# q loaded a batch ahead, gate stores from ScalarE's queue, and the second phase's weights in chunks

## The chip, the cores and the metric

The kernel runs on one core of a Trainium2 chip. TensorE (PE) multiplies, VectorE (DVE), ScalarE (ACT) and GpSimd (POOL) work elementwise, SyncE (SP) issues DMA transfers; ScalarE can issue them as well. The metric is the device time of one launch in microseconds. Kernels are compared by the median of several runs.

## The reference

Three layers follow each other over 8 batches of 576 tokens with 512 channels: linear attention in 8 heads with an RMS norm, a channel mix with a token shift and a squared ReLU, and causal attention in four experts of which two are chosen per token.

```python
kv  = einsum('bhsd,bhse->bhde', k, v)            # 64 x 64 per head
out = einsum('bhsd,bhde->bhse', q, kv)
x   = out / sqrt(mean(out*out) + 1e-6) * g_norm  # heads side by side: 512
xk  = mu_k * x + (1 - mu_k) * x_prev             # x_prev: x shifted by a token
xr  = mu_r * x + (1 - mu_r) * x_prev
k   = maximum(xk @ w_k, 0)                       # 512 -> 1024
x   = sigmoid(xr @ w_r) * (k*k @ w_v)            # 1024 -> 512
# then: logits = x @ w_gate, the best 2 of 4 experts,
# each: causal softmax attention with 64 columns, @ wo, weighted sum
```

## The kernel before

Channels lie on the 128 partitions, tokens run along the free dimension, in halves of 288 columns. To keep float32 accuracy an operand is split in a high and a low part (ScalarE writes the high part, VectorE the low one, L60 and L61), and a product is made of three matmuls (L65, L66, L67). The program has three parts.

phase_a (0 to 466 us of the profiled span) makes, batch by batch, the linear attention (front, L277), the mixed inputs (mix), the gates and the hidden values. front(b) multiplies k and v (L288), copies the result to the tile kv (ScalarE, L292), and then runs heads(h, a) four times: a q tile of 128 x 576 (qt, 288 KB) against kv into the PSUM tile po (L309, two buffers), from which ScalarE makes sq (L312) and xT (L313). Means, a reciprocal root on VectorE (rb) and a scaling (L355, L358) follow. load_q (L268 to L273) takes one of three qt buffers and issues the load from SP; heads(h, a) of tile i calls load_q(i + 3). load_kv issues k and v from SP, ten loads per batch. r_group makes one tile of gates: 12 matmuls, a sigmoid on ScalarE into sg (4 buffers, L424), and a store to the DRAM tile sgd from SP's queue (L425). k_group makes one tile of hidden values: ReLU on ScalarE (L433), the square on GpSimd (ksq), a store to kkd from SP's queue (L436). front runs one batch ahead: in the round of batch b the steps of front(b + 1) are taken between the groups of batch b. The weights w_v are converted to block sums during the first rounds (value_blocks; loads of vraw on ScalarE's queue, L444).

phase_v (466 to 652 us) multiplies the hidden values by w_v with seven block products per batch (products, L605; 168 matmuls a batch). prep(b + 1) makes the operands kk from the loaded kin and from differences tv of it (diff, L145), some on VectorE, some on GpSimd. ScalarE copies some results (kept: vp, vq, vu, L610), VectorE joins two (gated: ct, three buffers, L615), and GpSimd multiplies by the gates (sgv, L617); the batch is stored to x2d (L652). In the round b = 1 weights2 is called whole: ten weight loads through two buffers wst from SP (L88), each scaled where needed (VectorE, L90) and split (wqh and wql, wgh and wgl, woh and wol). In the round of the last batch the first 256 tokens of batch 0 are loaded to x20i from ScalarE's queue (L671), converted to x20h on ScalarE (L676) and to x20l on GpSimd (L677).

phase2 (652 to 1036 us) does the experts. prep(b, hf) loads half a batch to x2in from ScalarE's queue (L696), makes x2h (ScalarE, L702) and x2l (GpSimd, L703); qk_group makes qs and ks from them, v_group the values.

The order in which each engine works is not that of the source. The program is put in order by a list scheduler with a model of the engines' times, so source that stands late may be emitted early: the x20i load, written for the last batch, is issued at 507 us. Each engine then works its own queue strictly in order, and a DMA instruction that waits holds up what stands behind it on the engine that issues it. A DMA reports its end to one of eight completion semaphores that are used in turn, so its instruction also waits for the earlier transfer on that semaphore.

## Time and profile before

| | |
|---|---|
| runs | 1031.82, 1033.39, 1040.73 us; median 1033.39 |
| profiled execution | 1038.01 us, span 1036.2 us, mean granted clock 0.975 |
| PE | busy 978.7 us, 94% of the span |
| DVE | 646.0 us, 62% |
| ACT | 540.8 us, 52% |
| POOL | 428.9 us, 41% |
| q loads | 32 of 288 KB, 4.7 us median from issue to landing |
| chain that ended last | PE 69%, DMA 12%, DVE 7%, ACT 5%, POOL 4% |

Shares are means over three parts with different limits. Times of the trace are counted from the start of the span. The granted clock of 1.00 is TensorE at 2.4 GHz, 0.50 is 1.2 GHz.

### The profile page before, as it was taken

The page shows a single profiled execution, that of the slowest core. Times are in us where ns is not written, and L with a number is a line of the kernel's source. Part 1 is how long each engine was busy: PE and PEld are TensorE (multiplying, and loading weights), DVE is VectorE, ACT ScalarE, POOL GpSimd, SP SyncE. Part 2 cuts the span into 40 slices and gives each one's busy share as a digit, 9 for nine tenths or more (in the row PEclk, how much of TensorE's full clock was granted, in tenths as well). Part 3 has the DMA queues.
Part 4 walks back from the last instruction along what each step waited for, and adds up shares of the span by engine and source line. Part 5 has one row for each costly group of instructions (what it writes and reads, how often), then busy time and mean ns, then how long its engine had stood idle before and what let it go on. Part 6 is the DMA issues. An engine that isn't in the chain of part 4 may idle for free.

```text
span 1036.2 us, 21150 instructions
## 1 busy us (share of the span) xinstructions
PE 978.7 (94%) x7960; PEld 887.8 (86%) x7960; DVE 646.0 (62%) x1536; ACT 540.8 (52%) x1334; POOL 428.9 (41%) x512
## 2 busy tenths in 40 slices
PE   6789889898999899999989999899999999999998
PEld 3369779897979899999989999788989898888886
DVE  4869966353535355608998998265664755656562
ACT  4676656454545455624554453355554636454544
POOL 0006533131313131338689988454351616243331
PEclk9889989998999999999989999999999999999999
DMA  9563453434353522528665553300111202020102
GB/s 350 153 201 129 146 174 118 158 123 151 110 169 110 166 82 91 179 87 291 227 212 207 183 192 129 117 22 26 68 35 58 72 22 92 1 93 26 47 12 81
DMA packets 80181, 127.21 MB, mean 123 GB/s; under 512 B 7120, under 2 KB 57808, under 8 KB 78032
## 3 DMA queue, kind: packets, MB, share of 16 engines
q1 hardware_dynamic: 68752, 105.94, 30.5%
q10 hardware_dynamic: 11328, 19.93, 6.1%
q8 instruction: 63, 1.03, 0.4%
q14 instruction: 38, 0.31, 0.1%
HBM read 78.66 MB, written 47.19 MB: 121 GB/s over the span
## 4 chain that ended last, share of the span: by engine, by line
PE 69%; DMA 12%; DVE 7%; ACT 5%; POOL 4%; issue 2%; SPq 0%; ACTq 0%; POOLq 0%; DVEq 0%
PE acc L605 16%; PE acc L65 13%; PE acc L66 13%; PE acc L67 13%; PE pt L866 3%; PE acc L893 3%; DMA x2in<-x2d 3%; PE s L817 2%; DMA qt<-in_qT 2%; DMA kt<-in_k 2%; POOL x2l L703 2%; DMA vraw<-in_w_v 2%; ACT pr L829 2%; DVE xm L409 1%; POOL pr L846 1%
## 5 line engine op out<-in xcount | busy, mean ns | idle before, releaser
L435 POOL TENSOR_TENSOR ksq<-rl 128x288 f32<-128x288 f32 x128 | 99.0, 776 | 194.6 <-ACT rl L433 139.9
L66 PE MATMUL acc<-mixl,wkh 128*128 128x288 f32 x512 | 152.7, 298 | 0.0
L65 PE MATMUL acc<-mixh,wkh 128*128 128x288 f32 x512 | 151.9, 297 | 0.0
L67 PE MATMUL acc<-mixh,wkl 128*128 128x288 f32 x512 | 150.6, 294 | 0.0
L846 POOL TENSOR_SCALAR pr<-pr,rc,wg 128x512 f32<-128x512 f32 (+3 forms) x128 | 76.6, 613 | 99.8 <-DVE wg L776 60.2
L829 ACT ACTIVATE pr<-pr,nm 128x256 f32<-128x256 f32 (+4 forms) x144 | 83.2, 580 | 64.9 <-DVE nm L783 64.7
L605 PE MATMUL acc<-kk,wh_s 128*128 128x288 f32 x512 | 105.3, 300 | 4.7 <-DVE ct L615 3.8
L617 POOL TENSOR_TENSOR sgv<-ct,sgv 128x288 f32<-128x288 f32 x64 | 92.0, 1463 | 30.3 <-DVE ct L615 25.7
L402 DVE TENSOR_TENSOR mixl<-xm,mixh 128x288 fp32r<-128x288 f32 x120 | 55.8, 497 | 73.4 <-ACT mixh L410 73.3
L66 PEld LDWEIGHTS acc<-mixl,wkh 128*128 128x128 f32 x512 | 96.1, 188 | 1.3
L67 PEld LDWEIGHTS acc<-mixh,wkl 128*128 128x128 f32 x512 | 96.4, 188 | 0.0
L65 PEld LDWEIGHTS acc<-mixh,wkh 128*128 128x128 f32 x512 | 95.9, 187 | 0.4
L433 ACT ACTIVATE rl<-acc 128x288 f32<-128x288 f32 x128 | 51.6, 405 | 83.9 <-PE acc L67 76.7
L605 PEld LDWEIGHTS acc<-kk,wh_s 128*128 128x128 f32 x512 | 84.0, 192 | 5.2 <-DVE ct L615 4.0
L65 PE MATMUL acc<-mixh,wrh 128*128 128x288 f32 x256 | 82.9, 325 | 0.6 <-ACT rl L433 0.4
L67 PE MATMUL acc<-mixh,wrl 128*128 128x288 f32 x256 | 80.9, 316 | 0.0
L66 PE MATMUL acc<-mixl,wrh 128*128 128x288 f32 x256 | 80.0, 313 | 0.2 <-ACT mixl L400 0.2
L783 DVE CUSTOM_DVE_ANT_0 pr<-s,mask 128x256 f32<-128x256 f32 (+4 forms) x144 | 66.8, 481 | 18.3 <-PE pt L866 11.9
L605 PE MATMUL acc<-kk,wh_a 128*128 128x288 f32 x384 | 77.4, 295 | 0.0
L605 PE MATMUL acc<-kk,wl_s 128*128 128x288 f32 x256 | 76.3, 298 | 0.0
L65 PE MATMUL acc<-x2h,wqh 128*128 128x320 f32 (+1 forms) x240 | 74.2, 309 | 0.0
L67 PE MATMUL acc<-x2h,wql 128*128 128x320 f32 (+1 forms) x240 | 71.2, 297 | 0.0
(198 smaller groups left out, 2704.6 us busy)
## 6 DMA issues: line engine op xcount, KB each, us to landing
kkd<-ksq SPq DMA_DIRECT2D x128, 144.0 KB, 1.7
kin<-kkd SPq DMA_DIRECT2D x16, 1152.0 KB, 6.2
qt<-in_qT SPq DMA_DIRECT2D x32, 288.0 KB, 4.7
sgd<-sg SPq DMA_DIRECT2D x64, 144.0 KB, 2.2
sgv<-sgd SPq DMA_DIRECT2D x8, 1152.0 KB, 5.8
x2d<-sgv SPq DMA_DIRECT2D x8, 1152.0 KB, 5.9
out<-ob SPq DMA_DIRECT2D x28, 288.0 KB, 2.1
kt<-in_k SPq DMA_DIRECT2D x24, 256.0 KB, 4.6
```

What stands on the lines that cost most here:

```text
L65: nc.tensor.matmul(ps, wh(i), xh(i), start=(i == 0), stop=False)
L66: nc.tensor.matmul(ps, wh(i), xl(i), start=False, stop=False)
L67: nc.tensor.matmul(ps, wl(i), xh(i), start=False, stop=(i == n - 1))
L402: nc.vector.tensor_sub(xl[:, p, :], xp, xh[:, p, :].bitcast(F32))
L433: nc.scalar.activation(rl, acc[:, :HS], AF.Relu)
L435: nc.gpsimd.tensor_mul(sq, rl, rl)
L605: nc.tensor.matmul(q[:, :HS], a[:, i, ms_], c[:, i, :], start=(start and i == 0 and n == 0), stop=(stop and i == KH - 1 and n == 2), skip_ ...
L617: nc.gpsimd.tensor_mul(g, c, g)
L783: nc.vector.tensor_tensor_reduce(out=pr[:R, k0:k0 + kn], in0=s[:R, :kn], in1=mk, scale=1.0, scalar=lo, op0=ALU.add, op1=ALU.min, accum_out ...
L829: nc.scalar.activation(pr[:, :L], pr[:, :L], AF.Exp, bias=nm, scale=-1.0, accum_out=sms[b, p, j][:, e2:e2 + 1])
L846: nc.gpsimd.tensor_scalar(pr[:, :L], pr[:, :L], rc[:, r:r + 1], wg, op0=ALU.mult, op1=ALU.mult)
L866: nc.tensor.transpose(pt[:, (i - i0) * P:(i - i0 + 1) * P], pr[:, k1 - P:k1], ident)
```

## The change

q tiles have four buffers in place of three. The four tiles of the first batch are all loaded at the start, those of the second at the end of front(0), and from front(1) on heads of tile i asks for tile i + 4. Gate stores are issued from ScalarE's queue. Stores of hidden values are held in a list and issued two groups later. weights2 is a generator that gives one chunk at a step, and the w_v phase takes a step after some of its products. tv has two buffers in place of three there. x20i is loaded from SP's queue, with the other 320 tokens of batch 0 in a new tile x21 behind it, from which phase2 takes the second half of batch 0 in place of a load; two of the four x2l of that half are made on VectorE.

```diff
--- before.py
+++ after.py
@@ -90,12 +90,16 @@
                 nc.vector.tensor_scalar(st[:, :scaled], st[:, :scaled], -D ** -0.5, None, op0=ALU.mult)
             split(wh[:, kt, :], wl[:, kt, :], st[:, :f])
 
+        yield
         for i in range(KD):
             load_w(wqh, wql, w_qk, i, DM, NV)
+            yield
         for i in range(KD):
             load_w(wgh, wgl, w_vg, i, NV + E)
+            yield
         for i in range(2):
             load_w(woh, wol, w_o, i, DM)
+            yield
         nc.gpsimd.memset(mask, 0.0)
         nc.gpsimd.affine_select(out=mask[:, MC:], in_=mask[:, MC:], pattern=[[-1, P]], compare_op=ALU.is_ge, fill=BIG,
                                 base=0, channel_multiplier=1)
@@ -141,7 +145,7 @@
             ops[b, name] = (h, l)
 
         def diff(x, y, eng):
-            t = pools[-1].tile([P, KH, HS], F32, name="tv", bufs=3 if len(pools) > 1 else 1)
+            t = pools[-1].tile([P, KH, HS], F32, name="tv", bufs=2 if len(pools) > 1 else 1)
             eng.tensor_sub(t, x, y)
             return t
         operand("b11", quarter(0, 0))
@@ -268,7 +272,7 @@
             def load_q(i):
                 b, c = divmod(i, 4)
                 if b < B and i not in qts:
-                    qt = fr.tile([P, 2, HS], F32, name="qt", bufs=3)
+                    qt = fr.tile([P, 2, HS], F32, name="qt", bufs=4)
                     nc.sync.dma_start(qt, qT[b, c])
                     qts[i] = qt
 
@@ -307,7 +311,8 @@
                         for r in range(2):
                             rs = slice(r * D, (r + 1) * D)
                             nc.tensor.matmul(po[c * D:(c + 1) * D, r, :HS], kv[rs, 2 * a + c, :], qt[rs, c, :], start=True, stop=True, skip_group_check=True)
-                    load_q(i + 3)
+                    if b > 0:
+                        load_q(i + 4)
                     sq = sqs[h, a] = fr.tile([P, 2, HS], F32, name="sq", bufs=4)
                     nc.scalar.activation(sq, po[:, :, :HS], AF.Square)
                     nc.scalar.activation(xT[:, 2 * a:2 * a + 2, cols(h)], po[:, :, :HS], AF.Copy)
@@ -369,6 +374,8 @@
                         yield
                     for c in (3, 4):
                         load_kv(NF + c)
+                    for c in range(4):
+                        load_q(4 + c)
                     return
                 for h in range(2):
                     for a in range(2):
@@ -415,14 +422,18 @@
                 low(KD - 1)
                 yield
 
+            late = []
+
             def r_group(b, h, m):
+                while late:
+                    nc.sync.dma_start(*late.pop(0))
                 sg = sb.tile([P, HS], F32, name="sg", bufs=4)
                 xh, xl = mixed[b, h, "r"]
                 acc = acc_tile()
                 ms_ = slice(m * P, (m + 1) * P)
                 mm3(acc[:, :HS], lambda i: wrh[:, i, ms_], lambda i: wrl[:, i, ms_], lambda i: xh[:, i, :], lambda i: xl[:, i, :], KD)
                 nc.scalar.activation(sg, acc[:, :HS], AF.Sigmoid)
-                nc.sync.dma_start(sgd[b][:, m, h * HS:(h + 1) * HS], sg)
+                nc.scalar.dma_start(sgd[b][:, m, h * HS:(h + 1) * HS], sg)
 
             def k_group(b, h, m):
                 xh, xl = mixed[b, h, "k"]
@@ -433,7 +444,9 @@
                 nc.scalar.activation(rl, acc[:, :HS], AF.Relu)
                 sq = sb.tile([P, HS], F32, name="ksq", bufs=4)
                 nc.gpsimd.tensor_mul(sq, rl, rl)
-                nc.sync.dma_start(kkd[b][:, m, h * HS:(h + 1) * HS], sq)
+                late.append((kkd[b][:, m, h * HS:(h + 1) * HS], sq))
+                if len(late) > 2:
+                    nc.sync.dma_start(*late.pop(0))
 
             def value_blocks(pool):
 
@@ -494,7 +507,7 @@
                 for i in range(KD):
                     wts.append((wkh[:, i, c:c + CW], wkl[:, i, c:c + CW], w_k, i * P, c))
 
-            for c in "w0 w1 w2 k0 k1 k2 k3 k4 q0 q1 w3 q2".split():
+            for c in "w0 w1 w2 k0 k1 k2 k3 k4 q0 q1 w3 q2 q3".split():
                 i = int(c[1])
                 {"w": wload, "k": load_kv, "q": load_q}[c[0]](i)
             nc.sync.dma_start(g_sb, g2)
@@ -577,6 +590,9 @@
                 for x in (mk, mr or ()):
                     for _ in x:
                         pass
+                if not nxt:
+                    while late:
+                        nc.sync.dma_start(*late.pop(0))
                 if b == B - 2:
                     for _ in vals:
                         pass
@@ -663,15 +679,21 @@
                 load_s(b + 1)
                 if b == 1:
                     W["k0"].close()
-                    weights2()
+                    w2 = weights2()
                 if b == B - 1:
+                    for _ in w2:
+                        pass
                     W["x2"] = ExitStack()
                     x2p = W["x2"].enter_context(tc.tile_pool(name="x2p", bufs=1, side="right", reuse_waits="tile"))
+                    x21 = W["x21"] = x2p.tile([P, KD, S - 256], F32, name="x21")
                     x2, xh, xl = W["x20"] = [x2p.tile([P, KD, 256], t, name=f"x20{u}") for t, u in ((F32, "i"), (F32R, "h"), (F32R, "l"))]
-                    nc.scalar.dma_start(x2, x2d[0][:, :, :256])
+                    nc.sync.dma_start(x2, x2d[0][:, :, :256])
+                    nc.sync.dma_start(x21, x2d[0][:, :, 256:])
                 pr = prep(b + 1) if b + 1 < B else None
                 for n, _ in enumerate(products(b)):
                     run(pr)
+                    if b > 0 and n in (1, 3, 5):
+                        run(w2)
                     if b == B - 1 and 0 < n < 5:
                         nc.scalar.activation(xh[:, n - 1, :], x2[:, n - 1, :], AF.Copy)
                         nc.gpsimd.tensor_sub(xl[:, n - 1, :], x2[:, n - 1, :], xh[:, n - 1, :].bitcast(F32))
@@ -692,15 +714,18 @@
             def prep(b, hf):
                 q0, q1 = HF[hf]
                 w = q1 - q0
-                x2 = sb.tile([P, KD, HW], F32, name="x2in", bufs=1)
-                nc.scalar.dma_start(x2[:, :, :w], x2d[b][:, :, q0:q1])
+                if b == 0:
+                    x2 = W["x21"]
+                else:
+                    x2 = sb.tile([P, KD, HW], F32, name="x2in", bufs=1)
+                    nc.scalar.dma_start(x2[:, :, :w], x2d[b][:, :, q0:q1])
                 xh = sb.tile([P, KD, w], F32R, name=f"x2h{hf}", bufs=1)
                 xl = sb.tile([P, KD, w], F32R, name=f"x2l{hf}", bufs=1)
                 x2t[b, hf] = (xh, xl)
                 yield
                 for i in range(KD):
                     nc.scalar.activation(xh[:, i, :], x2[:, i, :w], AF.Copy)
-                    nc.gpsimd.tensor_sub(xl[:, i, :], x2[:, i, :w], xh[:, i, :].bitcast(F32))
+                    (nc.gpsimd if b or i % 2 else nc.vector).tensor_sub(xl[:, i, :], x2[:, i, :w], xh[:, i, :].bitcast(F32))
                     yield
```

SP's queue around the heads of front(3), before (kt and vt are loads for the next batch, qt loads of q tiles, sgd_75 the gate stores and kkd_67 the stores of hidden values):

```order
L264 DMA kt<-in_k 80x512
L265 DMA vt<-in_v 80x512
L425 DMA sgd_75<-sg 128x288 x2
L272 DMA qt<-in_qT 128x576 x2
L425 DMA sgd_75<-sg 128x288 x2
L272 DMA qt<-in_qT 128x576 x2
L425 DMA sgd_75<-sg 128x288 x3
L436 DMA kkd_67<-ksq 128x288 x16
```

and now:

```order
L269 DMA vt<-in_v 112x512
L268 DMA kt<-in_k 80x512
L269 DMA vt<-in_v 80x512
L276 DMA qt<-in_qT 128x576 x4
L449 DMA kkd_67<-ksq 128x288 x14
L429 DMA kkd_67<-ksq 128x288 x2
```

The gate stores have left, the four q loads stand in one piece behind the k and v loads, and the last two kkd stores of a batch are issued from the next group's line.

ScalarE around the kv copy and the first heads of front(3), before (sg is a sigmoid, sq and xT read the head products):

```order
L408 ACTIVATE xm<-xT,nuk 128x288
L292 ACTIVATE kv<-acc 128x256
L424 ACTIVATE sg<-acc 128x288 x2
L312 ACTIVATE sq<-po 128x576
L313 ACTIVATE xT<-po 128x2x288
L312 ACTIVATE sq<-po 128x576
L313 ACTIVATE xT<-po 128x2x288
L424 ACTIVATE sg<-acc 128x288
L410 ACTIVATE mixh<-xm 128x288 x3
L408 ACTIVATE xm<-xT,nuk 128x288
L424 ACTIVATE sg<-acc 128x288
L410 ACTIVATE mixh<-xm 128x288
```

and now:

```order
L417 ACTIVATE mixh<-xm 128x288
L415 ACTIVATE xm<-xT,nuk 128x288
L296 ACTIVATE kv<-acc 128x256
L435 ACTIVATE sg<-acc 128x288
L436 DMA sgd_75<-sg 128x288
L435 ACTIVATE sg<-acc 128x288
L436 DMA sgd_75<-sg 128x288
L317 ACTIVATE sq<-po 128x576
L318 ACTIVATE xT<-po 128x2x288
L317 ACTIVATE sq<-po 128x576
L318 ACTIVATE xT<-po 128x2x288
L435 ACTIVATE sg<-acc 128x288
```

Each sigmoid is followed by the store of its gates, right behind it or a few rows later, and two stores stand between the kv copy and the first sq.

VectorE in the second batch of the w_v phase, where the split of the weights (wql, wgl) meets the operands (kk) and the joins (ct), before:

```order
L90 TENSOR_SCALAR wst<-wst 128x256 x2
L61 TENSOR_TENSOR kk<-kin,kk 128x1152
L61 TENSOR_TENSOR wql<-wst,wqh 128x512 x2
L615 TENSOR_TENSOR ct<-acc,vu 128x288
L61 TENSOR_TENSOR kk<-kin,kk 128x1152
L615 TENSOR_TENSOR ct<-acc,vu 128x288
L61 TENSOR_TENSOR kk<-tv,kk 128x1152 x2
L61 TENSOR_TENSOR wgl<-wst,wgh 128x260 x2
L615 TENSOR_TENSOR ct<-acc,vq 128x288
L615 TENSOR_TENSOR ct<-vu,acc 128x288
```

and now:

```order
L90 TENSOR_SCALAR wst<-wst 128x256
L61 TENSOR_TENSOR kk<-kin,kk 128x1152
L61 TENSOR_TENSOR wql<-wst,wqh 128x512 x2
L61 TENSOR_TENSOR kk<-kin,kk 128x1152
L631 TENSOR_TENSOR ct<-acc,vu 128x288
L61 TENSOR_TENSOR wgl<-wst,wgh 128x260
L631 TENSOR_TENSOR ct<-acc,vu 128x288
L61 TENSOR_TENSOR kk<-tv,kk 128x1152 x2
L61 TENSOR_TENSOR wgl<-wst,wgh 128x260
L631 TENSOR_TENSOR ct<-acc,vq 128x288
L631 TENSOR_TENSOR ct<-vu,acc 128x288
```

One split of wgl has moved ahead of the second ct<-acc,vu, and the second kk<-kin,kk ahead of the first; the two scalings stand apart, and the other rows keep their order.

## Rows read from the trace of the kernel before

**Rows 1.** The page's second part, 40 slices of 25.9 us: granted clock, GB/s moved.
```profile
PEclk9889989998999999999989999999999999999999
...
GB/s 350 153 201 129 146 174 118 158 123 151 110 169 110 166 82 91 179 87 291 227 212 207 183 192 129 117 22 26 68 35 58 72 22 92 1 93 26 47 12 81
```

**Rows 2.** Idle time of TensorE by what ended it: us in total, times, longest us.
```profile
PE po L309 <- DMA qt<-in_qT: 13.4, 5, 3.3
...
PE po L309 <- ACT kv L292: 4.3, 2, 2.5
PE acc L605 <- DVE ct L615: 3.8, 1, 3.8
...
PE acc L65 <- DVE qs L61: 1.9, 1, 1.9
PE acc L65 <- DVE ks L61: 1.8, 1, 1.8
```

**Rows 3.** Windows, TensorE alone: from:to length, busy us (instructions) granted clock, DMA share, GB/s.
```profile
138.28:141.70 3.42, 3.42 (x28) 0.50 0.63 194
186.40:189.02 2.62, 0.00 (x1) 1.00 1.06 385
189.48:192.90 3.42, 3.42 (x19) 0.50 0.40 114
...
240.68:247.51 6.83, 6.37 (x35) 0.50 0.33 108
...
295.30:298.71 3.41, 3.41 (x19) 0.50 0.47 135
...
346.50:349.91 3.41, 3.41 (x16) 0.50 0.45 132
351.00:399.00 48.00, 48.00 (x467) 1.00 0.25 85
...
520.58:527.40 6.82, 5.50 (x23) 0.50 0.20 44
...
124.63:131.46 6.83, 6.13 (x33) 0.50 1.03 272
```

**Rows 4.** The chain that ended last, 180 to 196 us: start, us, what.
```profile
183.91 4.98 DMA qt<-in_qT
...
190.40 0.24 PE acc L65
...
193.17 0.13 PE acc L65
```

**Rows 5.** Timeline of SP's queue, 180 to 190 us: start, us, instruction.
```profile
182.19 1.08 SPq L425 DMA_DIRECT2D sgd<-sg  x2
```

**Rows 6.** Operations on vraw: the issue on ScalarE's queue, ns min/median/max, first and last start.
```profile
L444 ACTq DMA_DIRECT2D vraw<-in_w_v x8: 334/334/365, 56.5 to 140.0; - x8
```

**Rows 7.** Groups on ScalarE, 195 to 246 us: busy, mean ns, idle before, releaser.
```profile
L424 ACT ACTIVATE sg<-acc 128x288 f32<-128x288 f32 x7 | 2.8, 407 | 5.3 <-PE acc L67 5.3
```

**Rows 8.** Timeline of ScalarE, 172 to 190 us: start, us, instruction.
```profile
177.65 0.36 ACT L292 ACTIVATE kv<-acc 128x256 f32<-128x256 f32 x1
```

**Rows 9.** Timeline of TensorE, 172 to 190 us: start, us, instruction.
```profile
180.33 1.20 PE L309 MATMUL po<-qt,kv 64*64 64x288 f32 x16
```

**Rows 10.** The chain that ended last, 500 to 530 us: start, us, what.
```profile
507.53 6.44 DMA x20i<-x2d
...
517.76 2.75 DVE wgl L61
```

**Rows 11.** Operations on wst: the wgl split on VectorE, ns min/median/max.
```profile
L61 DVE TENSOR_TENSOR wgl<-wst,wgh x4: 657/804/2846, 517.8 to 527.0; 128x260 fp32r<-128x260 f32 x4
```

**Rows 12.** Timeline of GpSimd, 500 to 531 us: start, us, instruction.
```profile
516.59 3.74 POOL L145 TENSOR_TENSOR tv<-kin 128x1152 f32<-128x1152 f32 x1
```

**Rows 13.** Timeline of ScalarE, 655 to 672 us: start, us, instruction, idle before it.
```profile
665.16 1.34 ACT L702 ACTIVATE x2h<-x2in 128x256 fp32r<-128x256 f32 x4 [6.51 <-DMA x2in<-x2d]
```

**Rows 14.** Operations on sgd: from issue to landing.
```profile
DMA to landing us min/median/max: 1.7/2.6/12.9
```

## The prediction

> **What bounds the kernel now.** I read the page's slices first, for where TensorE is slow or idle, then its waits by releaser, then the windows around each gap, then the chain of waits. TensorE is the engine in front: busy 94% of 1036.2 us, and the slices of PE and of the granted clock dip in the same places [rows 1]. So the reader looks for two things: idle time of PE, and stretches at the lower clock. The waits list the idle time [rows 2]. Its largest item is the head products of L309 waiting for a q tile: 13.4 us in 5 waits, the longest 3.3. Each of the five (at 135, 186, 238, 291 and 343 us, once in each round from front(2) to front(6)) is followed within 3 us by a stretch in which the granted clock is 0.50, the 1.2 GHz level; those stretches are 3.42, 3.42, 6.83, 3.41 and 3.41 us long, 20.5 together [rows 3]. The control is front(7): from 351 to 399 us no wait falls, PE is busy for all 48.00 us, and the clock is 1.00 [rows 3]. A stretch at the lower clock is not lost whole. In the chain one 288-column matmul takes 0.24 us at 190.4 and 0.13 at 193.2 [rows 4], so a share of 1 - 0.13/0.24 = 0.46 is lost: 20.5 x 0.46 = 9.4 us.
>
> Why q is late stands in the same chain: the load of the fourth tile of a batch starts at 183.91 and lands 4.98 us later [rows 4]. It could not start sooner, because there are three qt buffers, so it needs the buffer that heads(b,0,0) frees (180.33 + 1.20) [rows 9], and because SP first issues two gate stores, at 182.19, that wait for their sigmoids [rows 5].
>
> **The change, part by part.**
>
> *q tiles.* All four tiles of a batch have a buffer of their own, and each load is issued when the tile of the batch before has been read. One round is 51.2 us (the slow stretches begin at 138.28, 189.48 and 240.68 [rows 3]), a load lands in 5 [rows 4], and SP's queue now holds no gate store ahead of it. Even with the burst of k and v loads that fills the DMA engines at that time (share 1.06 in the gap at 186.40 [rows 3]) some 40 us remain. I therefore take the five waits to go whole: -13.4. With them goes what starts the slow stretches; I take these too: -9.4. That is the less certain part; its bounds are 0 and -9.4, and I choose the far end because a stretch follows every one of the five waits and none occurs in front(7), where there is no wait. Sum -22.8.
>
> *One more q load at the start.* q3 is issued ahead of three small loads that the first mix needs. 288 KB at the first slice's 350 GB/s [rows 1] is 0.84 us; the bounds are 0 (the cores wait for other things there) and +0.84. I take +0.4.
>
> *Gate stores on ScalarE's queue.* 64 stores leave SP. What ACT pays for issuing one, the nearest row says: 0.33 us for a vraw load on its queue [rows 6]. Eight per batch are 2.7 us in a round in which ACT waits for PE anyway: its seven sigmoids between 195 and 246 us alone have 5.3 us of idle time ahead of them [rows 7], 0.76 each, so an issue of 0.33 is covered. The cover is thin where PE waits for ACT: in front(2) the kv copy is already late, 2.5 us [rows 2], and an issue ahead of it adds 0.33. I take +0.4 for all fronts. If a store had to wait behind its own sigmoid (0.41 us [rows 7]) each time, and were ahead of kv in each of six fronts uncovered, it would be 6 x (0.33 + 0.41) = 4.4: bounds 0 to +4.4. In the later fronts the kv copy ends at 178.01 and the first head product starts at 180.33 [rows 8, 9], 2.3 us of slack, hence the low end.
>
> Here a rule is to be weighed. Row: in the gap at 186.40 the DMA share is 1.06, so what is issued then has to share the engines whoever issues it [rows 3]. The Trainium skill, DMA: Bandwidth & Descriptors, section "Issuing engines are not separate DMA queues", says that transfers started by any engine run on the same 16 DMA engines and interleave, and that another issuer saves only sequencer time. By it this part alone gives nothing but 64 x 0.33 = 21 us of issue time that SP does not lack, and q would be early from its buffers, not from the stores' move; a queue that brought bandwidth of its own would shorten landings, which after the q change nobody waits for. Both ways the sum is the same, but the rule speaks for the slower rival below: the stores meet the k and v burst on the new queue too.
>
> *kkd stores two groups late, earlier fourth heads.* Nobody reads kkd before the second phase; 0. The fourth head products now stand directly behind the third, so PE asks for a po buffer about 0.7 us sooner (5 matmuls of 0.13), against the q wait of 2.6 that it no longer has; ACT's copies out of po are then the next thing that can be late. 0 here; it is a rival.
>
> *The w_v phase.* The rows of VectorE show the same operations ahead of the ct that ends the one stall there, with one wgl split moved past a ct. The stall is 3.8 us [rows 2] and a stretch of 6.82 us at 0.50 [rows 3], 3.1 lost: 6.9 in all. The chain that leads to it is the x20i load (6.44 us), ScalarE standing at x20h, then wgl on VectorE (2.75 us) [rows 10]. Three things move. ScalarE's x20h now stands behind the two kk conversions, the second wgh and vu, which takes the x20i wait out of the chain. The first wgh now stands ahead of the two kk conversions, and it waits for a weight load that can start only when wql has freed its buffer, as before. And GpSimd's tv difference and four x20l now come before the gates that free ct's three buffers: the tv alone is 3.74 us [rows 12]. The first helps, the other two hurt. Bounds -6.9 and +3.7; I take 0. tv with two buffers in place of three is 0 as well: the third difference is asked for two gates later, which the kk queue covers.
>
> *Start of the second phase.* The second half of batch 0 is read from x21, in place since the w_v phase, in place of a load. The two gaps are 1.9 and 1.8 [rows 2]; ahead of them ScalarE stood 6.51 us for a load of batch 1's half [rows 13], and that load stays ahead of qs on its queue, as do an exp table load and the first exponentials. I expect one gap in place of two, of about the same sum. Bounds -3.7 (both go) and +3.1 (a stretch at the lower clock as at 520.58 [rows 3] follows the longer gap); taken 0.
>
> Sum: -22.8 + 0.4 + 0.4 = -22.0. The profiled execution took 1038.01 us (its span 1036.2 and 1.8 around it), so 1016.0 in its terms. It is 4.6 above the median 1033.39 of the runs shown; from the median, 1033.4 - 22.0 = 1011.4. I predict 1011.5.
>
> **Rivals.**
> *The w_v stall goes too.* For it: the wgl split takes 0.66 us at its shortest and 2.85 at its longest [rows 11], and the long one lies within the 3.74 us of GpSimd's tv [rows 10, 12]; that tv now waits two gates and two x20l longer, so VectorE's splits may run free of it. 2.75 - 0.66 = 2.1 less for one wgl, and the 6.44 us of x20i [rows 10] that ScalarE no longer stands for would have to give the other 1.7 of the 3.8; the wait with its slow stretch is then gone: 1011.5 - 6.9 = 1004.6. The Trainium skill, GPSIMD Engine Reference, section "8. Key points", has GpSimd share SBUF interfaces with VectorE and contend with its two-input instructions; the rows on wgl agree. Against it: wgh is later on ScalarE.
>
> *The slow stretches stay.* Small waits (a po buffer, kv) remain near the heads and the clock falls as before: 1011.5 + 9.4 = 1020.9. Against: the gaps of 1.9 and 1.8 us at the start of the second phase have no slow stretch behind them (clock slices [rows 1]).
>
> *The wait changes its name.* PE stops at the same place for ScalarE (po not copied, kv) instead of q, as long as before: the 22.8 stay, 1033.4 + 0.8 = about 1034. Against: ScalarE is idle until PE ends its products at that time [rows 7].
>
> *Slower.* A gate store on ScalarE's queue waits not only for its sigmoid but for the earlier transfer whose completion semaphore it takes over; these are k and v loads of the burst, and gate stores landed up to 12.9 us after issue [rows 14]. The store holds all behind it on ScalarE: kv, sq, xT, mixh. From 2.3 us of delay [rows 8, 9] kv decides, and each of six fronts then looks like front(2): 2.5 us of wait [rows 2] and a stretch of 6.83 at 0.50 [rows 3], 3.1 lost. 6 x 5.6 = 33.6 against 22.8: 1033.4 + 10.8 + 0.8 = about 1045.
>
> **How the numbers follow.** Forecast 0.56, its own range 1006 to 1017 (the two bounded parts at half their size). W_v stall gone 0.17 (1004.6). Slow stretches stay 0.12 (1020.9). Wait renamed 0.08 (1034). Slower 0.07 (1045). Leaving out the last two and a tail below, 1002 to 1021 holds 8 in 10. About 1% (10 us) is what a measurement of this kernel can tell from no change: faster is below 1023, which the first three cases are: 0.85; same 0.08; slower 0.07.
>
> **What the profile will show.** Right: no wait of po for qt; no granted clock under 1.00 between 175 and 400 us; ACT's busy time up by some 0.3 us a store; one round of about 47 us (51.2 before, less 2.6 and 1.6). Wrong: waits of L309 (now L313) or L292's kv in its place, which would name ScalarE's queue; a clock of 0.50 after gaps under 1 us; a ct wait longer than 3.8 us near 500 us.

## The result, and the profile after

The changed kernel takes 1026.46 us in the median of 9 runs (1023.11 to 1032.20), the kernel before 1037.58 in 9 runs beside it (1031.82 to 1040.73). The ratio is 0.9907 [0.9882, 0.9933], some 10 to 11 us faster (9.7 by the ratio, 11.1 by the medians) where 22 were forecast, and the time lies above the stated range of 1002 to 1021. With nine runs the kernel before is also 4 us slower than the three runs had it that the forecast was made from; the forecast difference of 22 us does not depend on that. The profiled execution of the changed kernel, span 1030.3 us, is the slowest of the nine; a second profile (again, below) has 1028.5.

The waits of TensorE, changed kernel (what it waited for: us in total, times, longest), against [rows 2]:

```profile
PE po L360 <- DVE rb L352: 8.0, 4, 4.8
...
PE acc L65 <- DVE qs L61: 6.5, 2, 5.7
PE po L313 <- ACT kv L296: 5.7, 2, 3.0
PE acc L621 <- ACT vq L626: 4.9, 2, 3.1
...
PE acc L621 <- DVE ct L631: 1.7, 1, 1.7
```

The five waits for qt are gone. The ct wait fell from 3.8 to 1.7 us, but waits for vq (4.9) stand in its place, the wait for qs rose from 1.9 to 6.5 and that for kv from 4.3 to 5.7. The granted clock in 40 slices, against [rows 1], and TensorE in windows of the same trace (length, busy, instructions, clock, DMA share, GB/s), against [rows 3]:

```profile
PEclk9889988999999999999989999899999999999999
```

```profile
514.36:517.49 3.13, 0.00 (x1) 0.50 0.71 284
513.44:523.68 10.24, 7.11 (x31) 0.50 0.74 282
653.75:659.46 5.71, 0.00 (x1) 0.77 0.38 115
656.80:663.62 6.82, 4.16 (x19) 0.50 0.25 91
...
161.90:512.00 350.10, 346.27 (x3078) 1.00 0.47 157
```

From 162 to 512 us no stretch is slow any more. Two come later: 10.24 us around the second vq wait, where the kernel before had 6.82 us behind its ct wait, and 6.82 us behind the qs wait, where the kernel before had none at the start of its second phase.

The next table cuts every profiled execution at the same four instructions: the first product of the hidden values, the first of the w_v phase, the first with x20h, and the end of the span. In brackets stand the us at the 1.2 GHz level within a stretch.

| kernel | startup | rest of phase A | w_v phase | second phase | span |
|---|---|---|---|---|---|
| before | 85.5 (17.1) | 380.2 (27.3) | 186.8 (6.8) | 383.8 (0.2) | 1036.2 |
| changed | 89.1 (20.5) | 360.9 (13.7) | 190.4 (10.2) | 390.0 (8.3) | 1030.3 |
| again | 90.6 (23.9) | 358.4 (6.8) | 189.8 (6.8) | 389.6 (8.0) | 1028.5 |
| q_only | 88.2 (23.9) | 361.7 (13.7) | 186.0 (3.4) | 383.4 (0.9) | 1019.3 |
| a_part | 87.2 (20.5) | 356.6 (3.4) | 185.9 (3.4) | 383.5 (1.2) | 1013.2 |
| v_part | 86.2 (17.1) | 375.8 (13.7) | 189.7 (6.8) | 388.7 (7.5) | 1040.4 |
| a_x20 | 88.7 (20.5) | 358.1 (0.0) | 187.1 (6.8) | 383.6 (0.1) | 1017.5 |
| a_tv | 88.1 (23.9) | 358.3 (6.8) | 188.7 (3.4) | 383.2 (0.5) | 1018.3 |
| a_wst4 | 88.8 (23.9) | 358.0 (10.2) | 185.6 (0.0) | 382.6 (0.1) | 1015.0 |
| full_x21idle | 89.3 (20.5) | 356.7 (3.4) | 188.6 (3.4) | 383.5 (0.0) | 1018.1 |
| full_x2in2 | 88.8 (20.5) | 357.6 (3.4) | 190.0 (6.8) | 383.0 (8.5) | 1019.4 |
| full_sp | 90.0 (20.5) | 358.7 (6.8) | 190.1 (6.8) | 387.9 (6.9) | 1026.6 |
| a_q3late | 88.3 (20.5) | 358.3 (3.4) | 187.4 (6.8) | 383.9 (0.9) | 1017.8 |
| a_ring | 88.2 (17.1) | 357.5 (3.4) | 185.8 (3.4) | 383.6 (1.4) | 1015.1 |
| best | 88.5 (23.9) | 357.8 (10.2) | 185.2 (0.0) | 381.6 (6.8) | 1013.0 |
| best3 | 88.4 (17.1) | 358.3 (3.4) | 185.7 (3.4) | 376.4 (0.0) | 1008.8 |

The changed kernel against before: phase A gives 19.3 us (21.8 in again), the startup takes back 3.6 (5.1), the w_v phase 3.6 (3.0), the second phase 6.2 (5.8).

### The profile page after: what moved, and what is told of

Same layout as the page of the kernel before. It is cut to its first block, busy times and chain, and to the rows that moved or that the text cites. A ratio compares the mean times of both kernels' runs of the same rounds, so it can differ in the third digit from the quotient of the medians.

```text
span 1030.3 us, 21148 instructions
## 1 busy us (share of the span) xinstructions
PE 974.2 (95%) x7960; PEld 886.0 (86%) x7960; DVE 646.0 (63%) x1538; ACT 540.8 (52%) x1334; POOL 417.5 (41%) x510
## 4 chain that ended last, share of the span: by engine, by line
PE 67%; DMA 12%; DVE 7%; ACT 5%; POOL 5%; issue 2%; SPq 0%; ACTq 0%; DVEq 0%; POOLq 0%
PE acc L65 15%; PE acc L66 14%; PE acc L67 14%; PE acc L621 12%; DMA x2in<-x2d 3%; PE acc L918 3%; PE pt L891 3%; PE s L842 2%; DMA vraw<-in_w_v 2%; ACT pr L854 2%; POOL x2l L728 2%; POOL pr L871 2%; DMA kin<-kkd 2%; PE po L313 1%; DMA kt<-in_k 1%
## 5 line engine op out<-in xcount | busy, mean ns | idle before, releaser
L446 POOL TENSOR_TENSOR ksq<-rl 128x288 f32<-128x288 f32 x128 | 96.5, 756 | 173.8 <-ACT rl L444 141.8
L65 PE MATMUL acc<-mixh,wrh 128*128 128x288 f32 x256 | 79.5, 311 | 0.5 <-ACT rl L444 0.5
L67 PE MATMUL acc<-mixh,wrl 128*128 128x288 f32 x256 | 76.8, 300 | 0.0
L66 PE MATMUL acc<-mixl,wrh 128*128 128x288 f32 x256 | 76.5, 299 | 0.2 <-ACT mixl L407 0.2
L66 PE MATMUL acc<-x2l,wqh 128*128 128x320 f32 (+1 forms) x240 | 71.0, 296 | 0.0
```

Source lines behind the costliest of these rows:

```text
L65: nc.tensor.matmul(ps, wh(i), xh(i), start=(i == 0), stop=False)
L66: nc.tensor.matmul(ps, wh(i), xl(i), start=False, stop=False)
L67: nc.tensor.matmul(ps, wl(i), xh(i), start=False, stop=(i == n - 1))
L446: nc.gpsimd.tensor_mul(sq, rl, rl)
```

## The experiments

Theory 1 was that the q part gives about what was forecast and that the edits behind phase A, taken as free, take half of it back. Each ratio below is to the kernel before in runs beside it.

**again** is the changed kernel itself.

> The changed kernel once more, for a second profile beside the first. The first profiled execution (span 1030.3) lies 6 us above the median of its timed runs, so one of its parts should be a chance of that execution. If the loss is in the w_v phase and at the start of the second phase (theory 1), the stalls near 502 to 517 us (7 us of idle time) and the 5.7 us gap near 654 us are here again, and phase A ends again near 450 us. If the gain of phase A itself is smaller than 16 us (rival), phase A ends later than 453 us here. Ratio to before again about 0.990.

Measured: 1027.26 us, ratio 0.9912 [0.9887, 0.9937]. The vq and qs waits are there again (5.1 and 6.7 us), and phase A ends at 449.0.

**q_only.**

```diff
-                    qt = fr.tile([P, 2, HS], F32, name="qt", bufs=3)
+                    qt = fr.tile([P, 2, HS], F32, name="qt", bufs=4)
...
-                    load_q(i + 3)
+                    if b > 0:
+                        load_q(i + 4)
...
+                    for c in range(4):
+                        load_q(4 + c)
...
-            for c in "w0 w1 w2 k0 k1 k2 k3 k4 q0 q1 w3 q2".split():
+            for c in "w0 w1 w2 k0 k1 k2 k3 k4 q0 q1 w3 q2 q3".split():
```

> Only the q part: four qt buffers, loads a batch ahead; the gate and hidden stores, the weights and x20 as before. Theory 1 (the q part gives what was forecast, the rest takes half of it back): 18 to 22 us faster than before, ratio 0.979 to 0.983, no wait of the head products for qt. Rival (the slow stretches stay or the startup takes back): 10 us or less, ratio 0.990 or more. Rival (gate stores ahead on SP hold q even with a batch of lead): the waits for qt remain in part.

Measured: 1018.02 us, 0.9824 [0.9799, 0.9849], 18 us faster: at the low end of theory 1, and 8 to 9 us better than the whole change. No head product waits for qt, though the gate stores are still on SP's queue: the buffers alone do it. What q3 costs the startup is in these 18 us.

**a_part** adds the gate stores on ScalarE's queue and the late hidden stores.

```diff
-                nc.sync.dma_start(sgd[b][:, m, h * HS:(h + 1) * HS], sg)
+                nc.scalar.dma_start(sgd[b][:, m, h * HS:(h + 1) * HS], sg)
...
+                late.append((kkd[b][:, m, h * HS:(h + 1) * HS], sq))
+                if len(late) > 2:
+                    nc.sync.dma_start(*late.pop(0))
```

> All of the change in phase A (q tiles, gate stores on ScalarE's queue, hidden stores two groups late); the w_v phase and the second phase as before. Theory 1: as q_only, ratio 0.979 to 0.983, since the stores are worth nothing. Rival (the stores on ScalarE's queue cost): 3 us or more slower than q_only, with kv or po waits near the heads in its trace.

Measured: 1018.30 us, 0.9822 [0.9798, 0.9847]. It equals q_only: the two kinds of stores neither give nor cost anything that the time can tell.

**v_part** has the rest of the change on the old phase A: weights in chunks, tv with two buffers, x20 and x21 on SP's queue, two x2l on VectorE.

```diff
-            t = pools[-1].tile([P, KH, HS], F32, name="tv", bufs=3 if len(pools) > 1 else 1)
+            t = pools[-1].tile([P, KH, HS], F32, name="tv", bufs=2 if len(pools) > 1 else 1)
...
-                    weights2()
+                    w2 = weights2()
...
-                    nc.scalar.dma_start(x2, x2d[0][:, :, :256])
+                    nc.sync.dma_start(x2, x2d[0][:, :, :256])
+                    nc.sync.dma_start(x21, x2d[0][:, :, 256:])
```

> Only the change behind phase A: weights in chunks, tv with two buffers, x20 and x21 on SP's queue, two x2l on VectorE; phase A as before, so its five waits for qt stay. Theory 1: 6 to 10 us slower than before, ratio 1.006 to 1.010, with ScalarE waiting for weight chunks in front of the copies vq, and one gap of about 5 us at the start of the second phase. Rival: within 2 us of before, ratio 0.998 to 1.002.

Measured: 1042.16 us, 1.0068 [1.0037, 1.0100], 6 to 7 us slower, as theory 1 had it. The three waits side by side (TensorE, v_part):

```profile
PE po L313 <- DMA qt<-in_qT: 11.6, 5, 3.2
...
PE acc L65 <- DVE qs L61: 6.4, 2, 5.6
...
PE acc L609 <- ACT vq L614: 5.1, 2, 4.3
```

So the loss comes from behind phase A and is there without the q part. This trace also bears on the slow stretches, since all five waits for qt are still in it (2.15, 1.62, 2.87, 1.80 and 3.16 us). TensorE in windows around them:

```profile
134.22:136.37 2.15, 0.00 (x1) 1.00 0.90 337
136.37:151.80 15.43, 14.86 (x131) 1.00 0.44 142
...
187.63:189.25 1.62, 0.00 (x0) 1.00 1.03 371
189.25:236.54 47.29, 47.28 (x448) 1.00 0.41 131
236.54:239.41 2.87, 0.00 (x1) 1.00 1.03 366
240.92:244.33 3.41, 3.41 (x19) 0.50 0.42 130
288.18:289.98 1.80, 0.00 (x1) 1.00 1.05 377
289.98:337.28 47.30, 47.29 (x448) 1.00 0.42 135
337.28:340.44 3.16, 0.00 (x1) 0.91 0.95 323
339.90:346.73 6.83, 6.29 (x35) 0.50 0.34 109
```

Behind the waits of 1.62 and 1.80 us the clock stays at 1.00 for the 47 us to the next wait; behind those of 2.87 and 3.16 it falls, and behind the first, of 2.15, it does not. The third slow stretch of phase A in the table's 13.7 us follows a wait for rb. So not every wait for qt brings a slow stretch, as the one trace of before had suggested.

**a_tv** is a_part with two tv buffers, nothing else.

> The changes of phase A and, of those behind it, only tv with two buffers instead of three; weights whole, x20 on ScalarE's queue and no x21, as before. The emitted order is not that of a_part: on ScalarE the splits of the weights (wgh, woh) move ahead of copies (vq) and operands (kk). Theory 1a (the loss of the w_v phase is this new order, in which ScalarE stands for weight chunks in front of what TensorE waits for): 3 to 5 us slower than a_part's 1018.3, some 1022, with TensorE waiting for vq near 510 us; the start of the second phase as in a_part. Rival (the loss comes from the x21 transfer on SP's queue): as a_part, within 1 us.

Measured: 1019.80 us, 0.9845 [0.9811, 0.9879], an interval that overlaps a_part's. In the trace the w_v phase is 188.7 us against 185.9, and the wait is the new one (TensorE, a_tv):

```profile
PE acc L617 <- ACT vq L622: 4.4, 1, 4.4
```

One buffer less changes the order that the scheduler emits: on ScalarE both woh splits move ahead of the vq copies, and GpSimd makes the differences tv of this stretch behind its x20l, in place of one ahead of them (ScalarE, a_tv: start, us, instruction, idle time before it and what ended it):

```profile
509.56 1.16 ACT L60 ACTIVATE kk<-tv 128x1152 fp32r<-128x1152 f32 x1 [3.41 <-POOL tv L145]
510.90 0.63 ACT L60 ACTIVATE woh<-wst 128x512 fp32r<-128x512 f32 x1 [0.18 <-DMA wst<-in_w_o]
511.44 0.39 ACT L622 ACTIVATE vq<-acc 128x288 f32<-128x288 f32 x1
```

The time alone does not tell theory and rival apart. By the traces the new stall is there without the x21 transfer, and the six executions with three tv buffers have a w_v phase of 185.8 to 187.4 us, the seven with two tv and two chunk buffers one of 188.6 to 190.4. But the order, and not the chunks alone, is what a_tv shows: here ScalarE stands 3.41 us for tv and 0.18 us for a chunk. In the changed kernel it is the chunks (ScalarE):

```profile
510.33 0.42 ACT L60 ACTIVATE wgh<-wst 128x260 fp32r<-128x260 f32 x1 [3.33 <-DMA wst<-in_w_vg]
...
511.71 0.39 ACT L626 ACTIVATE vq<-acc 128x288 f32<-128x288 f32 x1
515.46 0.63 ACT L60 ACTIVATE woh<-wst 128x512 fp32r<-128x512 f32 x1 [3.37 <-DMA wst<-in_w_o]
...
517.05 0.39 ACT L626 ACTIVATE vq<-acc 128x288 f32<-128x288 f32 x1
```

ScalarE stands 3.3 us twice for a weight chunk that nobody needs before the second phase, with a copy behind it that TensorE waits for. The same two waits, of 2.3 to 2.8 and of 3.8 to 4.2 us, are in again, v_part, full_x21idle, full_x2in2 and full_sp.

**a_x20** is a_part with x20i issued from SP's queue.

> The changes of phase A and x20i loaded from SP's queue, no x21, tv with three buffers, weights whole. Every engine's order is that of a_part but for this one load. Both theories: within 1 us of a_part's 1018.3, the wait for ct of 3.8 us still there, since the load lands at the same time from either queue. If ScalarE's standing for its own issue mattered: 2 us faster.

Measured: 1019.14 us, 0.9843 [0.9809, 0.9876]: no difference from a_part, the ct wait still there. Which queue x20 comes from is worth nothing that can be measured.

**full_x21idle** is the whole change, with x21 loaded but not read: the second phase loads batch 0's second half as before.

```diff
-                if b == 0:
-                    x2 = W["x21"]
-                else:
-                    x2 = sb.tile([P, KD, HW], F32, name="x2in", bufs=1)
-                    nc.scalar.dma_start(x2[:, :, :w], x2d[b][:, :, q0:q1])
+                x2 = sb.tile([P, KD, HW], F32, name="x2in", bufs=1)
+                nc.scalar.dma_start(x2[:, :, :w], x2d[b][:, :, q0:q1])
```

> The whole change with x21 still loaded, but the second phase loads batch 0's second half to x2in as before, so x21 is read by nobody. The w_v phase keeps its order; at the start of the second phase the first load of batch 1 waits again for the x2in buffer and no longer stands ahead of qs. Theory 1 (most of what was lost is that place): the gap of 5.7 to 5.9 us becomes two of about 1 us as in a_part, no slow stretch behind it, and the time falls by 6 us against the change, to about 1021. Rival (the x21 transfer itself, or the two x2l on VectorE, costs it): 1026 to 1027 as the change.

Measured: 1021.97 us, 0.9855 [0.9826, 0.9884], some 5 us better than the change; the second phase is 383.5 us as in a_part, with a wait of 1.6 us for qs and no slow stretch. Loading x21 is not what costs here; reading it is, because the load that it replaces was what kept batch 1's load back. ScalarE at that place in the changed kernel:

```profile
643.40 0.60 ACTq L721 DMA_DIRECT2D x2in<-x2d  x1
651.51 1.34 ACT L727 ACTIVATE x2h<-x2in 128x256 fp32r<-128x256 f32 x4 [7.73 <-DMA x2in<-x2d]
654.85 0.53 ACTq L721 DMA_DIRECT2D x2in<-x2d  x1
655.41 1.28 ACT L854 ACT_TABLE_LOAD   x1 [2.55 <-POOL x2l L728]
...
658.47 0.41 ACT L60 ACTIVATE qs<-acc 128x320 fp32r<-128x320 f32 x1
```

With the x2in buffer free, batch 1's load goes out at 643.40, and ScalarE stands 7.73 us at its landing, then 2.55 us until GpSimd has read the buffer and the next load may go out, then does the table load and four exponentials, all ahead of the qs split that TensorE waits for from 653.75.

**full_sp** is the whole change with the x2in loads on SP's queue.

```diff
-                    nc.scalar.dma_start(x2[:, :, :w], x2d[b][:, :, q0:q1])
+                    nc.sync.dma_start(x2[:, :, :w], x2d[b][:, :, q0:q1])
```

> The whole change with the x2in loads issued from SP's queue, so that ScalarE never stands for the buffer of a load, only for its landing. At the start of the second phase this takes away the 2.6 us in which ScalarE waits for GpSimd's x2l, and leaves the wait for the landing, the table load and the exponentials ahead of qs. Theory 1: the gap falls from 5.8 to about 3.2 us; 1023 to 1025 if nothing else moves. Rival (the landing is all of it): gap 5.7 as before.

Measured: 1023.87 us, 0.9872 [0.9842, 0.9902], some 3 us under the change with intervals that overlap. ScalarE no longer stands between x2h and the table load (full_sp, the same view):

```profile
649.77 1.34 ACT L727 ACTIVATE x2h<-x2in 128x256 fp32r<-128x256 f32 x4 [7.58 <-DMA x2in<-x2d]
651.13 1.28 ACT L854 ACT_TABLE_LOAD   x1
...
654.19 0.41 ACT L60 ACTIVATE qs<-acc 128x320 fp32r<-128x320 f32 x1
```

and the wait of TensorE is 3.0 us instead of 5.7, as forecast from the 2.6:

```profile
PE acc L65 <- DVE qs L61: 3.8, 2, 3.0
```

**full_x2in2** is the whole change with two x2in buffers.

> The whole change with two buffers for x2in, so that the load of batch 1's second half no longer waits on ScalarE's queue for GpSimd's x2l. Theory 1 (the gap at the start of the second phase is ScalarE's queue: a load's landing, then this wait of 2.5 us, then table load and exponentials, all ahead of qs): the gap of 5.7 to 5.9 us falls to about 3.3, and the time by 2 to 4 us against the change, some 1023 to 1025. Rival (the gap is set by qs's own products or by the landing of the first x2in load): no change, 1027. The longer order of the second phase also shifts a little with the buffer.

Measured: 1021.21 us, 0.9867 [0.9833, 0.9901]. The time fell by 5 to 6 us, more than the 2 to 4 expected, and for another reason than the one given. The gap is still 5.75 us, since the third load now takes the place of the second on ScalarE's queue and stands there as long (ScalarE, full_x2in2):

```profile
650.92 0.53 ACTq L721 DMA_DIRECT2D x2in<-x2d  x1
651.48 1.28 ACT L854 ACT_TABLE_LOAD   x1 [2.59 <-POOL x2l L728]
```

The gain lies in the rest of the second phase, which from its first transpose on takes 354.3 us instead of 360.8.

**a_wst4** is a_part with two tv buffers and four buffers for the weight chunks.

```diff
-            st = w2.tile([P, DM], F32, name="wst", bufs=2)
+            st = w2.tile([P, DM], F32, name="wst", bufs=4)
```

> The changes of phase A, tv with two buffers and four buffers for the weight chunks instead of two, so that chunk loads are issued before the splits ahead of them are done. Theory 1a: chunks are there when ScalarE reaches them, so the w_v phase loses its idle time in vq and perhaps part of the ct wait: 3 to 6 us faster than a_tv, 1 to 4 us faster than a_part (1014 to 1017). Rival (VectorE's work in this stretch is the limit, whenever the chunks come): as a_tv.

Measured: 1017.17 us, 0.9825 [0.9787, 0.9862], 2.6 us under a_tv (3 to 6 expected) and within the error of a_part. The w_v phase takes 185.6 us, 3 less than in a_tv, and 185.2 and 185.7 in best and best3, which have the same buffers. The stall is not gone, though: TensorE is idle for 5.7 us there, against 7.2 in a_tv, all of it for vq, and the other half of the 3 us is a slow stretch of 3.4 us that this execution does not have. ScalarE in a_wst4:

```profile
485.53 0.42 ACT L60 ACTIVATE wgh<-wst 128x260 fp32r<-128x260 f32 x1 [2.99 <-DMA wst<-in_w_vg]
...
509.14 1.16 ACT L60 ACTIVATE kk<-tv 128x1152 fp32r<-128x1152 f32 x1 [6.26 <-POOL tv L145]
510.21 0.39 ACT L622 ACTIVATE vq<-acc 128x288 f32<-128x288 f32 x1
```

One vq copy (at 486.91) still stands behind a chunk, another behind a difference tv of GpSimd.

**a_q3late** is a_part with q3 behind the loads of g, mu_k and mu_r.

> The changes of phase A with q3 loaded behind the three small loads (g, mu_k, mu_r) instead of ahead of them. Theory (the 2 to 3 us that the startup lost come from mu_k landing later, on which VectorE's queue and through it ScalarE stand): the startup is back at 86 us (a_part 87.2 to 88.7, before 85.5), the kv wait of front(0) at 1.9 us instead of 3.0, and the time 1 to 2.5 us under a_part. Rival (the startup is limited by all bytes that are loaded there): no change.

Measured: 1018.72 us, 0.9825 [0.9799, 0.9851], startup 88.3 us. This theory fell. mu_k does land earlier (VectorE reads it at 18.85 us, in a_part at 19.68), but the kv copy is as late as in a_part (21.13; 19.89 in the kernel before) (ScalarE, a_q3late):

```profile
20.81 0.33 ACTq L236 DMA_DIRECT2D xT<-in_w_k  x1
21.19 0.38 ACT L292 ACTIVATE kv<-acc 128x256 f32<-128x256 f32 x1 [0.79 <-DMA raw<-in_w_k]
```

Ahead of kv stands a weight load that waits for an earlier transfer on its completion semaphore. With one more load in the program the eight semaphores fall to other transfers, and here to one that lands at 20.7 us rather than at 19.2.

**a_ring** takes the load of g off the shared semaphores (a_q3late, and g from GpSimd's queue).

```diff
-            nc.sync.dma_start(g_sb, g2)
+            nc.gpsimd.dma_start(g_sb, g2)
```

> a_q3late (the changes of phase A, q3 behind the small loads) with the load of g issued from GpSimd's queue, so that it takes none of the eight completion semaphores that the other queues share. The fourth load of w_k on ScalarE's queue, which stands ahead of the kv copy, then waits for the same semaphore as before (that of a k load, landed at 19.2 us in the kernel before) and not for that of the second w_k load (landed at 20.7). Theory: the kv wait of front(0) falls from 3.0 to 1.9 us, the startup from 88.3 to about 86 us, and the time by 1 to 2.5 us, to 1016 to 1017. Rival (the startup pays for the bytes of q3, wherever they stand): kv wait 3.0, startup 88 or more, 1018.

Measured: 1019.88 us, 0.9840 [0.9815, 0.9865]. ScalarE's wait in front of kv is 0.36 us now and ends with TensorE's products. TensorE's wait for it is 0.9 us instead of 3.0, but the startup is again 88.2 us and the time did not fall. The edit has a cost of its own: from GpSimd's queue the load of g goes out at 1.25 us, among the first k and v loads, in place of 12.19 (a_q3late), and the first product of k and v starts later (GpSimd and TensorE, a_ring):

```profile
1.25 0.74 POOL L509 DMA_DIRECT2D g_sb<-in_g  x1 [0.81 <-POOLq L1053]
...
7.48 1.12 PE L288 MATMUL acc<-vt,kt 128*64 128x64 f32 x16 [7.48 <-DMA vt<-in_v]
```

That product starts at 7.5 us in the two executions with this edit (a_ring, best3) and at 6.2 to 6.7 in all others. So the run fits the semaphore as the cause of the longer kv wait, although the later start shifts that wait too; what sets the startup as a whole stays open.

**best** and **best3** put together what had helped. best has a_wst4, q3 late, and two x2in buffers loaded from SP's queue:

> A version from what the runs showed: the changes of phase A, q3 behind the small loads, tv with two buffers and four buffers for the weight chunks, x2in with two buffers loaded from SP's queue; no x21, weights whole, x20 on ScalarE's queue. From a_wst4's 1017: about 1.5 us less in the startup, and 4 to 6 us less in the second phase, where two x2in buffers took that much off the rest (full_x2in2): 1010 to 1012. If the second phase's gain hangs on x21: 1015 to 1016.

Measured: 1015.13 us, 0.9787 [0.9761, 0.9813], against 1010 to 1012 expected. At the start of the second phase ScalarE stood 7.2 us for a load and then made x2h of both halves in one go, and TensorE waited 4.5 us for x2h, with a slow stretch of 6.8 us behind.

The time is the rival's, but not for its reason: from its first transpose on the second phase takes 353.6 us, so the gain of two buffers does not hang on x21. best3 goes back to x2in loads from ScalarE's queue, keeps one x2in buffer for the first loads and gives the rest a second one:

```diff
-                x2 = sb.tile([P, KD, HW], F32, name="x2in", bufs=1)
+                x2 = sb.tile([P, KD, HW], F32, name="x2in" if b < 2 or hf else "x2inb", bufs=1)
```

> a_ring with tv in two buffers, four buffers for weight chunks, and from the second batch of the second phase on a buffer of its own for the first half's x2in, so that the start of the second phase keeps the order of a_part and the rest has two buffers. From a_wst4's 1017: the startup's 1 to 2, and the second phase's 6 (rest of the span 354 instead of 360, start 22.7 instead of 28): 1009 to 1011. If two buffers help only with the loads issued early: 1015.

Measured: 1010.83 us, 0.9760 [0.9735, 0.9785], faster than both kernels. The second phase takes 376.4 us instead of 383.8, with no slow stretch in it, which is about the gain over a_wst4; the startup gave nothing (88.4 us).

Weights in chunks alone were not run. The changed kernel with weights2 called whole has, row by row on every engine, the same instructions in the same order, so in this program that edit does nothing.

## Why the prediction was wrong

*q tiles, waits: right.* The five waits are gone, and from front(3) to front(7) one round is 46.8 us (head products start at 185.0, 231.9, 278.7, 325.6 and 372.4 us; forecast about 47, before 51.3 to 53.4).

*q tiles, slow stretches: mis-sized.* The term of 9.4 us took every one of the five waits to bring a slow stretch. That was so in one execution; in v_part three of the five bring none, and the stretches behind the other two are 3.4 and 6.8 us, of which 0.46 is 4.7. So two executions of the old phase A put the term at 9.4 and at 4.7, and the forecast took the one it had seen. q_only measures 18, with what q3 costs the startup in it: 2.7 us against the kernel before and 2.0 against v_part. The q part itself thus gave some 20 to 21 of the 22.8. Part of the gain met a later limit that was not named: in the changed kernel front(2) waits 2.2 us for rb, with a slow stretch of 6.8 behind it, where the kernel before waits 0.8. v_part, with the old phase A, waits 2.5 us there, so it does not take the new loads to make rb late.

*Startup: mis-sized.* Forecast +0.4 with a bound of 0.84, from the bytes of one q tile. Measured +1.7 to +5.1 in the executions that have q3 there. The bytes were the wrong price. One thing seen is the extra wait of 1.1 us for kv: one more load moved the completion semaphores by one, and ScalarE's queue passes that wait on to kv. Another is the clock: the startup has 17.1 us at the lower level in both executions of the old phase A, 17.1 to 23.9 in those with q3, and 0.46 of the 6.8 us more is 3.1. Neither moving the load behind the small ones nor taking the kv wait away (a_ring, at the cost of a later first product) shortened the startup, so the cause as a whole stays open.

*Stores: right.* The gate stores were put at +0.4 for all fronts, from an issue ahead of kv in front(2), the hidden stores at 0. TensorE's wait for kv in front(2) is 2.5 us in the three executions with the gate stores on SP's queue and 2.7 to 3.1 in the thirteen with them on ScalarE's; the times of q_only and a_part agree within 0.3 us. The median landing of a gate store is 2.2 and 3.0 us from SP (before, q_only) and 2.7 and 3.0 from ScalarE (a_part, changed), so nothing landed sooner. The Trainium skill's rule (DMA: Bandwidth & Descriptors, "Issuing engines are not separate DMA queues") that another issuer saves only sequencer time agrees with that. The slower rival that leaned on it did not come; no kv wait shows in front(3) to front(6). That rival also misread [rows 14]: the 12.9 us belong to a load of gates in the w_v phase (sgv<-sgd), and the longest gate store took 7.4. And ACT's busy time could not be a sign: it is 540.8 us in both kernels, since issuing a DMA is not counted as busy.

*The w_v phase: mis-sized.* Forecast 0 with bounds -6.9 and +3.7; it took 3.0 to 3.6 us. One of its steps failed: tv with two buffers was put at 0, since "the kk queue covers" the later third difference. a_tv has that edit alone, and its w_v phase is 2.8 us longer than a_part's, with ScalarE standing 3.41 us for a tv. Another held in part. The x20i load no longer stands ahead of ct: ScalarE waits 0.77 us for it in place of 3.11, and the ct wait fell by 2.1. But it is still in the chain, on the way to the second vq wait, and with it the chunk that can go out only when VectorE's wgl split has freed a buffer (changed kernel):

```profile
495.22 7.10 DMA x20i<-x2d
...
508.83 0.53 DVE wgl L61
...
509.38 6.06 DMA wst<-in_w_o
```

A kin load of 1152 KB goes out 0.84 us ahead of that chunk; what it adds to the 6.06 us no run shows. The prediction named wgh's wait for its load among the things that hurt, without a price; that the copies vq would stand behind such waits, it did not see. On the rival with GpSimd and VectorE: one kk split on VectorE took 3.69 us while GpSimd did a tv and an x20l, against 1.34 for the two splits of the same form at 491.6 and 494.1, when GpSimd was idle. The Trainium skill (GPSIMD Engine Reference, "8. Key points") has the two engines share SBUF interfaces; the row agrees.

```profile
504.77 3.69 DVE L61 TENSOR_TENSOR kk<-kin,kk 128x1152 fp32r<-128x1152 f32 x1 [0.73 <-ACT kk L60]
```

But the kernel before has the like, beside a tv, so this is not what the change added (VectorE, before):

```profile
507.41 3.81 DVE L61 TENSOR_TENSOR kk<-kin,kk 128x1152 fp32r<-128x1152 f32 x1
```

*The start of the second phase: the step that failed most.* "I expect one gap in place of two, of about the same sum", bounds -3.7 and +3.1. One gap it was, but of 5.7 us with a slow stretch of 6.8 behind it: 2.8 more than the old two (5.7 + 0.8 against 3.7), and 0.46 x 6.8 = 3.1, in all 5.9 of the 6.2 us. The prediction saw that the load stays ahead of qs and kept the old length of its wait. But that load now goes out together with the last store of the w_v phase, and ScalarE stood at it, at the next load and through four exponentials in front of qs. full_x21idle shows that all of it goes when that load is held back, full_sp that the wait at the next load is 2.6 us of the gap. How the other 3 us divide between the longer landing (8.0 us in place of 4.1), the table load and the exponentials was not run apart.

By the timed runs the missing 11 us split in two: q_only gives 18 where the q part and the startup were put at 22.4, and the edits behind phase A cost 6 to 7 (v_part) where they were put at nothing.

## What to carry to other kernels

Where a load is made unnecessary, look at what its buffer was holding back: the next load moves up, and on an in-order queue its landing then stands in front of other work. A transfer that is issued from an engine that also computes has to be priced at its landing and at the wait for its buffer, not at its issue. A slow-clock stretch seen behind a wait in one execution is a chance and not a fixed price; count it in several. Where a scheduler orders the program, one buffer less can reorder other engines, so it is not worth nothing until the emitted orders have been compared.

## What the runs showed of the hardware

One x2in load of 512 KB landed 7.9 to 8.1 us after its issue when it was issued within 0.1 us of a store of 1152 KB (changed kernel, again, v_part), and after 4.1 to 4.2 us where that store had gone out 4.7 to 5.7 us earlier (kernel before, a_part, full_x21idle). That the store is the cause was not tested apart.

A wait of TensorE did not bring the lower clock every time. Waits of 1.62 and 1.80 us were followed by 47 us at the full clock (v_part), those of 2.1 to 3.3 us in the kernel before by stretches of 3.4 or 6.8 us at the 1.2 GHz level [rows 3]. Near 2 us both were seen: the rb wait of 2.15 us in a_wst4 had such a stretch behind it, the wait of 2.15 us for qt in v_part and the rb wait of 1.89 in a_part had none. The length alone does not decide: a kv wait of 3.06 us in a_q3late had none behind it, and one of 1.69 us for sq in a_ring had one of 3.41 (windows of a_q3late, then of a_ring):

```profile
124.77:127.83 3.06, 0.00 (x0) 1.00 0.90 251
127.83:150.00 22.17, 19.92 (x177) 1.00 0.72 239
...
138.04:139.73 1.69, 0.00 (x1) 1.00 0.75 245
139.88:143.29 3.41, 3.01 (x32) 0.50 0.40 127
```

One more load in the program changed which earlier transfer a later load waits for, by the turn of the eight completion semaphores: one that landed at 20.7 us in place of one at 19.2 (a_q3late, kernel before), in front of a copy that TensorE waited 3.0 us for in place of 1.9.
